# A scan followed by two mixture-of-experts layers: how many empty row blocks the ACT queue writes per unit of work

## The chip, the cores and the metric

The kernel runs on one core of one Trainium2 chip. The metric is the device time of one execution in microseconds (us); lower is better. The core has five engines with an instruction queue each: PE (matrix multiply), DVE (vector), ACT (activations; it also issues DMAs), POOL and SP (which here only issues DMAs). A queue is worked off in order: an instruction that waits holds up everything behind it on that engine.

## What is computed

```python
for t in range(S):                       # x is 2 x 5056 x 256
    h = f[:, t] * h + i[:, t] * x[:, t]  # gated scan, y[:, t] = h
x = y.reshape(10112, 256)
x = moe(x, cosine router, w1, w2)        # layer 0
out = moe(x, linear router, w1, w2)      # layer 1
# moe: expert e = argmax of 8 logits per row, gate = softmax probability of e
#      out[row] = gate * (relu(x[row] @ w1[e]) @ w2[e]),  w1: 256 x 1024, w2: 1024 x 256
```

## The kernel before

**Rows sorted by expert.** Each layer has a table in DRAM, `X[0]` and `X[1]`, with a region for every expert that would hold all rows. The scan and the router of layer 0 write each row, and the router of layer 1 each output row of layer 0, to the next free slot of its expert, by indirect DMAs of POOL. A layer's work is cut into tiles of 128 rows of one expert. The number of rows of an expert is known only at the end, so a layer is planned in phases: while rows still arrive, only full tiles are planned; when the last row has been counted, `checkpoint(..., final=True)` plans the rest, among them one partly filled tile for each expert. What lies behind an expert's last row must then be defined, so for each of the eight experts a block of 128 rows (`zrow`, 129 KB, zeros with an invalid row number) is written just behind its last row. These eight writes per layer are the subject of the change.

**Units.** A tile needs two units, one for each half of the 1024 hidden columns. A unit is `mm1` (L827, 24 matmuls of 128 columns into one PSUM buffer `hps`), `evac` (ACT makes the high half of `hT` with a relu at L835, DVE the low half at L188), and three units later `mm2` (L849, 12 matmuls of 256 columns, `hT` times `W2`, into a PSUM buffer `ops`). Most tiles run their two units one after the other; the last 21 tiles of layer 0 and the first 21 of layer 1 run all first halves and then all second halves, with the partial sum copied out by ACT (`acc`, L853), while the weights of one half are exchanged. Six PSUM buffers are shared by `hps`, `ops`, the scan's transposes and the transposes `x2p` of layer 1's router.

**Order of the work.** Python builds a list of slots, one for each unit; a function put into slot i with a priority writes its instructions there. Within a slot: `do_loads` (1), `mm1` (5), `pad_rows` (13), router steps and weight parts, `evac` (50), `mm2` (55). From slot 17 on the order on PE, ACT, SP and POOL is this written order; that on DVE is chosen by a scheduler when the kernel is built. ACT also loads weights (512 KB each from `w1b`, `w2b` into `ws`, L384, three buffers) and converts them (L397, L419).

**The empty blocks.** `checkpoint` computes the eight addresses on DVE (`pads`), and puts the eight calls into the slots behind its own:

```python
for e in range(E):                                             # E = 8, L715
    at(now[0] + 1 + e // cfg["padn"], 13, pad_rows, m, pads, e)
```

```python
def pad_rows(m, pads, e):                                      # L703
    if e == 0:
        A.load(preg, pads[0:1, 0:E])                           # addresses into ACT's registers
        ...
    x_write(m, A.dma_start(out=X[m][ds(pval[m, e], P), :], in_=zrow[0]), "Xp")
```

`x_write` says what need not be ordered: all other writes to `X[m]` are declared independent of the blocks. The blocks are not declared independent of each other (the address is a register's value), so each block's DMA waits, at ACT, until the one ahead has landed. The loads of tiles that the final plan made (`t_load`, L802, on SP) wait for all eight (`x_read`); tiles of earlier phases don't.

Of the kernel before, what the change touches and what calls it, by code (L numbers as in the profile page):

```python
# [117 lines left out]
 't0at': (-3, 40),  # L118
 'w1at': (16766, 49534),
 'w2at': (82048, 114816),  # L120
 'padn': 1,
 'xq': 'S'}


# [1315 lines left out]
```

## Time and profile before

| | |
|---|---|
| three runs | 1076.33, 1081.48, 1098.4 us; median 1081.48 |
| the profiled execution's own time | 1075.63 us |
| its span, first to last instruction | 1073.8 us |
| busy share of the span: PE, DVE, ACT, POOL | 93%, 56%, 49%, 40% |
| mean granted clock of PE | 0.981 |

How to read it: the span is shorter than the time by 1.83 us around it. The final plan of layer 0 stands at about 425 us of the span, that of layer 1 at about 650 us. PE is busy nearly always, so time is lost or won where PE stands still, and a share of busy time of another engine says little; what counts is whether PE waits for it.

### The profile page before, as it was taken

The page shows a single profiled execution, that of the slowest core. Times are in us where ns is not written, and L with a number is a line of the kernel's source. Part 1 is how long each engine was busy: PE and PEld are TensorE (multiplying, and loading weights), DVE is VectorE, ACT ScalarE, POOL GpSimd, SP SyncE. Part 2 cuts the span into 40 slices and gives each one's busy share as a digit, 9 for nine tenths or more (in the row PEclk, how much of TensorE's full clock was granted, in tenths as well). Part 3 has the DMA queues.
Part 4 walks back from the last instruction along what each step waited for, and adds up shares of the span by engine and source line. Part 5 has one row for each costly group of instructions (what it writes and reads, how often), then busy time and mean ns, then how long its engine had stood idle before and what let it go on. Part 6 is the DMA issues. An engine that isn't in the chain of part 4 may idle for free. (4 is left out here: it accounts for less than half of the span.)

```text
span 1073.8 us, 37047 instructions
## 1 busy us (share of the span) xinstructions
PE 1003.0 (93%) x13267; PEld 933.6 (87%) x13267; DVE 604.3 (56%) x2007; ACT 525.3 (49%) x1301; POOL 432.7 (40%) x864
## 2 busy tenths in 40 slices
PE   4557999999999999889999999899999999999997
PEld 4436889999999998779999998899999999999997
DVE  8989767787778776556429876543222222222221
ACT  6888455655555654456336564543333333333332
POOL 4276756667776665222101551143222222222222
PEclk9967999999999999989999999999999999999999
DMA  9699425876665773555459589843322222222220
GB/s 352 204 331 236 120 68 115 136 142 115 130 134 135 137 120 91 154 156 151 108 113 259 121 173 219 157 100 84 55 55 51 51 51 52 46 52 44 46 51 31
DMA packets 195616, 132.72 MB, mean 124 GB/s; under 512 B 169601, under 2 KB 172558, under 8 KB 195440
## 3 DMA queue, kind: packets, MB, share of 16 engines
q1 hardware_dynamic: 170080, 58.07, 27.5%
q10 hardware_dynamic: 13504, 40.74, 15.3%
q0 software_dynamic: 11856, 31.51, 11.0%
q8 instruction: 118, 1.93, 0.8%
q14 instruction: 58, 0.48, 0.2%
HBM read 58.89 MB, written 38.85 MB: 91 GB/s over the span
## 5 line engine op out<-in xcount | busy, mean ns | idle before, releaser
L827 PE MATMUL hps<-xT,W 128*128 128x128 f16 x7968 | 508.4, 220 | 16.7 <-DVE hT L188 5.8
L827 PEld LDWEIGHTS <-W 128*128 x7968 | 476.5, 98 | 29.5 <-issue 16.3
L849 PE MATMUL ops<-W,hT 128*128 x3984 | 492.5, 273 | 2.8 <-ACT W L397 1.0
L188 DVE SCALAR_TENSOR_TENSOR hT<-hps,hT 128x512 f16<-128x512 f32 x332 | 228.3, 688 | 343.3 <-ACT hT L835 325.9
L849 PEld LDWEIGHTS <-hT 128*128 128x128 f16 x3984 | 375.1, 98 | 44.1 <-issue 4.1
L835 ACT ACTIVATE hT<-hps 128x512 f16<-128x512 f32 x332 | 197.7, 596 | 336.9 <-PE hps L827 258.5
L1017 POOL DMA_INDIRECT out<-osum,ti x83 | 81.3, 979 | 301.2 <-ACT osum L1013 176.6
L995 POOL DMA_INDIRECT X<-trow,tsl x83 | 98.4, 1186 | 49.5 <-DVE tsl L188 16.4
L690 POOL DMA_INDIRECT X<-row,sl x79 | 88.8, 1124 | 69.8 <-issue 25.3
L1013 ACT ACTIVATE osum<-ops,exr 128x256 f32<-128x256 f32 x62 | 29.4, 474 | 47.0 <-PE ops L849 44.8
L196 POOL TENSOR_TENSOR lf<-exr,us 128x2 f32<-128x2 f32 (+1 forms) x42 | 9.5, 226 | 105.2 <-DVE us L192 52.0
L188 DVE SCALAR_TENSOR_TENSOR W<-ws,W 128x1024 f16<-128x1024 f32 x34 | 41.4, 1221 | 7.3 <-ACT W L397 7.2
L531 PE MATMUL yt<-cs,xf 128*128 128x128 f32 x126 | 27.9, 299 | 16.2 <-DVE xf L516 13.6
L516 DVE TENSOR_TENSOR_SCAN xf<-xf 128x256 f32<-128x256 f32 (+3 forms) x64 | 42.7, 708 | 0.1
L397 ACT ACTIVATE W<-ws 128x1024 f16<-128x1024 f32 x35 | 36.9, 1058 | 9.1 <-DMA ws<-w1b 5.0
L872 ACT ACTIVATE trow<-osum 128x256 f16<-128x256 f32 x83 | 35.1, 423 | 12.4 <-DMA X<-trow,tsl 4.9
L861 ACT ACTIVATE osum<-ops 128x256 f32<-128x256 f32 x58 | 22.2, 382 | 35.4 <-PE ops L849 29.0
L188 DVE SCALAR_TENSOR_TENSOR trow<-osum,tsc,trow 128x256 f16<-128x256 f32 x83 | 37.4, 481 | 3.3 <-ACT trow L887 1.7
L533 PEld LDWEIGHTS yt<-cs,xf 128*128 128x128 f32 x252 | 35.3, 204 | 0.8 <-issue 0.7
L188 DVE SCALAR_TENSOR_TENSOR row<-yt,sc,row 128x256 f16<-128x256 f32 x79 | 36.0, 472 | 0.0
L887 ACT ACTIVATE trow<-osum,tsc 128x256 f16<-128x256 f32 x62 | 28.1, 500 | 14.8 <-DVE tsc L193 11.9
L571 ACT ACTIVATE row<-yt,sc 128x256 f16<-128x256 f32 x79 | 33.1, 478 | 3.2 <-DVE sc L193 3.2
(161 smaller groups left out, 956.6 us busy)
## 6 DMA issues: line engine op xcount, KB each, us to landing
xf<-xf ACTq DMA_DIRECT2D x28, 512.0 KB
ws<-w1b ACTq DMA_DIRECT2D x16, 512.0 KB
ws<-w2b ACTq DMA_DIRECT2D x16, 512.0 KB
W<-w1a SPq DMA_DIRECT2D x11, 512.0 KB
W<-xf SPq DMA_DIRECT2D x8, 512.0 KB
ws<-w2a ACTq DMA_DIRECT2D x8, 512.0 KB
WD<-wq SPq DMA_DIRECT2D x8, 512.0 KB
W<-WD SPq DMA_DIRECT2D x8, 512.0 KB
```

Of the source, the lines that this page charges most:

```text
L188: return eng.scalar_tensor_tensor(out=out, in0=in0, scalar=s, in1=in1, op0=op0, op1=op1, **kw)
L397: A.activation(out=hi, in_=src, func=ACTF.Copy, scale=64.0)
L516: V.tensor_tensor_scan(out=t[:, k, lo:hi], data0=t[:, 2 + k, lo:hi], data1=t[:, k, lo:hi], initial=init, op0=ALU.mult, op1=ALU.subtract)
L533: T.matmul(out=yt[:, D:D + E], lhsT=t[:, k, i * P:(i + 1) * P], rhs=ide[:, (1 - k) * (P + E):(1 - k) * (P + E) + E], start=(k == 0), stop= ...
L571: A.activation(out=p["row"][:, o + i, 0:D], in_=yv(d["yt"][i]), func=ACTF.Copy, scale=p["sc"][:, o + i:o + i + 1])
L690: x_write(0, G.indirect_dma_start(out=X[0], out_offset=IndirectOffsetOnAxis(ap=p["sl"][:, i, 0:1], axis=0), in_=p["row"][:, i, :].bitcast( ...
L827: T.matmul(out=hps[:, c, :], lhsT=w, rhs=xt[:, a, :], start=(n == 0), stop=(n == 5))
L835: A.activation(out=hh[:, 0], in_=hps, func=ACTF.Relu)
L849: T.matmul(out=o, lhsT=hT[:, a + k, :], rhs=w[:, b * D:(b + 1) * D], start=(first and k == 0 and n == 0), stop=(last and k == 3 and n == 2))
L872: A.activation(out=d["row"][:, i, D:2 * D], in_=t["O"], func=ACTF.Square, scale=0.25, accum_out=d["ss"][:, i:i + 1])
L995: x_write(1, G.indirect_dma_start(out=X[1], out_offset=IndirectOffsetOnAxis(ap=sl[:, i, 0:1], axis=0), in_=d["row"][:, i].bitcast(I32), in ...
L1017: i = ins_of(G.indirect_dma_start(out=out, out_offset=IndirectOffsetOnAxis(ap=ti, axis=0), in_=r, in_offset=None, bounds_check=N - 1, oob_ ...
```

## The change

One number in the table of settings: the eight blocks of a layer are written four in the first slot behind the final plan and four in the second, not one in each of eight slots. This holds for both layers.

```diff
- 'padn': 1,
+ 'padn': 4,
```

On ACT in layer 0, from the loading of the addresses (`pads`) on, the queue before has one block (`X_99<-zrow`), the high half of `hT` of that unit, two copies of transposes (`x2p`), a weight load and the second block. The names after "waits" are semaphores; DMAHW ones count landed DMAs.

```order
L705 TENSOR_LOAD pads [waits DVE_49]
L708 ISA
L708 DMA X_99<-zrow 128x258 [waits DMAHW4_49]
L835 ACTIVATE hT<-hps 128x512 [waits PE_49]
L923 ACTIVATE x_11125<-x2p 128x512 [waits DMAHW2_49,DMAHW1_49,DMAHW6_49,DMAHW0_49,PE_49]
L923 ACTIVATE x_11127<-x2p 128x512 [waits DMAHW2_49,DMAHW7_49,DMAHW1_49,PE_49]
L384 DMA ws<-w1b 128x1024
L708 ISA
L708 DMA X_99<-zrow 128x258 [waits DMAHW4_49,DMAHW0_49]
```

The same place on ACT now:

```order
L708 DMA X_99<-zrow 128x258 [waits DMAHW4_49]
L708 ISA
L708 DMA X_99<-zrow 128x258 [waits DMAHW6_49,DMAHW4_49]
L708 ISA
L708 DMA X_99<-zrow 128x258 [waits DMAHW6_49,DMAHW0_49]
L708 ISA
L708 DMA X_99<-zrow 128x258 [waits DMAHW1_49,DMAHW0_49]
L835 ACTIVATE hT<-hps 128x512 [waits PE_49]
L923 ACTIVATE x_11128<-x2p 128x512 [waits DMAHW2_49,PE_49]
L923 ACTIVATE x_11130<-x2p 128x512 [waits DMAHW7_49,DMAHW2_49,PE_49]
L384 DMA ws<-w1b 128x1024 [waits DMAHW2_49]
```

Three more blocks stand ahead of `hT`, the two copies and the weight load; four more follow behind that load, ahead of the next unit's `hT`.

On ACT in layer 1, between the first and the second unit behind the plan, the queue before has one block (`X_100<-zrow`) for each `hT`, weight part (L397), weight load (L384) and partial sum (L853).

```order
L835 ACTIVATE hT<-hps 128x512 [waits PE_49]
L397 ACTIVATE W_1_105<-ws 128x4x256 [waits DMAHW0_49]
L384 DMA ws<-w2b 128x1024 [waits DMAHW5_49,DVE_49]
L853 ACTIVATE acc_17990<-ops 128x256 [waits PE_49]
L708 ISA
L708 DMA X_100<-zrow 128x258 [waits DMAHW3_49]
L835 ACTIVATE hT<-hps 128x512 [waits PE_49]
```

The same place on ACT now:

```order
L835 ACTIVATE hT<-hps 128x512 [waits PE_49]
L397 ACTIVATE W_1_105<-ws 128x4x256
L384 DMA ws<-w2b 128x1024 [waits DMAHW1_49,DVE_49]
L853 ACTIVATE acc_17993<-ops 128x256 [waits PE_49]
L708 ISA
L708 DMA X_100<-zrow 128x258 [waits DMAHW0_49]
L708 ISA
L708 DMA X_100<-zrow 128x258 [waits DMAHW4_49,DMAHW3_49]
L708 ISA
L708 DMA X_100<-zrow 128x258 [waits DMAHW7_49,DMAHW4_49]
L708 ISA
L708 DMA X_100<-zrow 128x258 [waits DMAHW7_49]
```

Four blocks stand ahead of the second `hT` where one stood, and as many ahead of the first. On PE, SP and POOL the order of the instructions is the same in both kernels (on PE only buffer numbers differ).

## Rows read from the trace of the kernel before

**Rows 1.** Busy time by engine over the whole span, from the page.
```profile
PE 1003.0 (93%) x13267; PEld 933.6 (87%) x13267; DVE 604.3 (56%) x2007; ACT 525.3 (49%) x1301; POOL 432.7 (40%) x864
```

**Rows 2.** Who waited for the block writes (tile zrow): line, total us, times.
```profile
  ACT hT L835: 17.0, 9
```

**Rows 3.** ACT's timeline, layer 0: start, us, engine, line, [idle before <-releaser]; ACTq issues.
```profile
427.33 0.38 ACTq L708 DMA_DIRECT2D X<-zrow  x1
...
440.15 0.42 ACT L872 ACTIVATE trow<-osum 128x256 f16<-128x256 f32 x1 [2.33 <-DMA X<-zrow]
...
443.29 0.34 ACTq L708 DMA_DIRECT2D X<-zrow  x1
...
443.94 0.35 ACTq L384 DMA_DIRECT2D ws<-w1b  x1
...
444.17 1.08 ACT L923 ACTIVATE x<-x2p 128x512 f16<-128x512 f16 x2
...
445.54 0.34 ACTq L708 DMA_DIRECT2D X<-zrow  x1
...
450.50 0.34 ACTq L708 DMA_DIRECT2D X<-zrow  x1
...
453.16 0.34 ACTq L708 DMA_DIRECT2D X<-zrow  x1
```

**Rows 4.** PE's timeline, layer 0, behind the final plan.
```profile
441.69 0.29 PE L915 MATMUL x2p<-id,trow 128*128 128x128 f16 x2 [0.64 <-DVE toh L188]
...
455.40 0.86 PE L915 MATMUL x2p<-id,trow 128*128 128x128 f16 x8 [1.50 <-ACT trow L887]
...
461.65 2.72 PE L827 MATMUL hps<-xT,W 128*128 128x128 f16 x24 [3.99 <-DMA xT<-X]
464.16 2.76 PE L849 MATMUL ops<-W,hT 128*128 x12
466.72 1.83 PE L827 MATMUL hps<-xT,W 128*128 128x128 f16 x24
```

**Rows 5.** SP's waits, 400 to 480 us: total us, times, longest.
```profile
SPq L802 <- DMA X<-zrow: 24.1, 1, 24.1
```

**Rows 6.** One window: us, busy of PE, PEld, DVE, ACT, POOL, granted clock, DMA share, GB/s.
```profile
462.00:467.00 5.00, 5.00 (x38) 4.20 (x36) 0.69 (x1) 0.63 (x2) 0.14 (x1) 0.50 0.53 102
```

**Rows 7.** ACT's timeline, layer 1.
```profile
656.63 0.36 ACTq L708 DMA_DIRECT2D X<-zrow  x1
...
659.78 1.06 ACT L397 ACTIVATE W<-ws 128x1024 f16<-128x1024 f32 x1 [2.15 <-DMA ws<-w2b]
...
660.74 0.36 ACT L853 ACTIVATE acc<-ops 128x256 f32<-128x256 f32 x1
...
663.15 0.36 ACTq L708 DMA_DIRECT2D X<-zrow  x1
...
668.17 0.39 ACTq L708 DMA_DIRECT2D X<-zrow  x1
...
668.60 0.60 ACT L835 ACTIVATE hT<-hps 128x512 f16<-128x512 f32 x1 [3.23 <-DMA X<-zrow]
...
670.66 0.39 ACTq L708 DMA_DIRECT2D X<-zrow  x1
```

**Rows 8.** PE's timeline, layer 1.
```profile
663.18 1.50 PE L827 MATMUL hps<-xT,W 128*128 128x128 f16 x24
664.52 1.47 PE L849 MATMUL ops<-W,hT 128*128 x12
665.83 1.50 PE L827 MATMUL hps<-xT,W 128*128 128x128 f16 x24
...
669.98 1.50 PE L827 MATMUL hps<-xT,W 128*128 128x128 f16 x24 [1.34 <-DVE hT L188]
...
688.56 1.51 PE L849 MATMUL ops<-W,hT 128*128 x12 [1.01 <-ACT W L397]
```

**Rows 9.** PE's waits, 645 to 700 us: total us, times, longest.
```profile
PE hps L827 <- DVE hT L188: 3.8, 3, 1.9
```

## The prediction

> **What bounds the kernel now.** The busy times come first: PE works 93% of the span, so time is won or lost only where PE stands still [rows 1]. Then I asked who waits for the changed writes: ACT stood before its `hT` activations for 17.0 us, nine times, until a block of empty rows had landed [rows 2]. Does PE feel that? In layer 0, SP's first load of a tile from the final plan waited 24.1 us for the blocks [rows 5], and PE ran out of tiles: it stood 3.99 us until 461.65 [rows 4]. The three groups after that took 2.72, 2.76 and 1.83 us, against 1.50, 1.47 and 1.50 elsewhere [rows 4, 8]: the clock granted from 462 to 467 us was 0.50, that is 1.2 instead of 2.4 GHz, after the stop and full again before 472 or so [rows 6]. The lower level cost 1.22 + 1.29 + 0.33 = 2.84 us. In layer 1 no tile came late, but PE waited 3.8 us, in three places, for `hT` halves that ACT made late [rows 9]; the one at 669.98 goes back to an `hT` at 668.60 that had stood 3.23 us behind a block [rows 7, 8].
>
> So the blocks have two prices: how late the last one lands (SP, layer 0), and how long ACT is held at once. The change lowers the first and raises the second.
>
> **What a block costs ACT.** A block is issued when the one ahead has landed, so the distance of two issues is the price where ACT had nothing else to do. Alone: 445.54 − 443.29 = 2.25, 453.16 − 450.50 = 2.66, 670.66 − 668.17 = 2.49 us [rows 3, 7]. Behind a 512 KB weight load on the same queue: 450.50 − 445.54 = 4.96 (the load was issued at 443.94), and in layer 1, where loads follow each other, 6.52 (656.63 to 663.15) and 5.02 (663.15 to 668.17) [rows 3, 7]. I take 2.5 alone and 4.96 behind a load, and keep 2.66 and 6.52 as the upper end.
>
> The trace's blocks differ by a factor of three at one size. The Trainium skill (DMA: Bandwidth & Descriptors, "Anatomy of one DMA") gives a write about 2.0 us plus its bytes at 436 GB/s; for 129 KB an estimate from that page is 2.30 us for any block. This agrees with the lone rows, and the row of 6.52 us speaks against it. What the rule would make of the time stands among the rivals.
>
> **Layer 0.** The queue up to the first block, 427.33, is unchanged. Three more at 2.5 each: the fourth is issued at 434.83. Issue 0.38, `hT` 0.60, the two `x2p` copies 1.08, weight load issue 0.35: 437.24; the fifth waits for the fourth's landing, 437.33. It stands behind that load: sixth at 442.29, seventh 444.79, eighth 447.29. Behind it stand the square of one output tile (0.42), two `hT` (1.20) and a copy (taken as 0.36, like `acc`), with the issue 0.38: the second square starts at 449.7 [rows 3, 7]. In the trace of before the second square starts at 440.15, and PE's transposes that need its row at 441.69, 1.54 us later [rows 3, 4]. So they start at 451.2: **+9.5 us**. Everything else PE has in between (about one unit, and the router's logits that wait for the copies) fits before that. PE stands still longer than before 461.65, so I add the lower clock once: +2.84.
>
> What goes: the eighth block lands near 450 to 452 instead of after 453.16, and PE reaches the first tile of the final plan some 9 us later. Its stop of 3.99 us goes, with the 2.84 us of clock behind it, and the 1.50 us at 455.40, where ACT's `trow` had waited for the last block [rows 4]. Net: 9.5 + 2.84 − 3.99 − 2.84 − 1.50 = **+4.0 us**.
>
> **Layer 1.** A new matmul group into `hps` needs the buffer of the group three units ahead (six buffers, two used by a unit). The wait at 669.98 shows the distance: `hT` at 668.60 on ACT, 1.38 us until PE starts (ACT 0.60, then DVE's half) [rows 7, 8]. First block 656.63, behind a load as before, so the second at 663.15; third 665.65, fourth 668.15. The `hT` behind it starts at 668.53, and PE's group of 663.18 starts at 669.91. Then ACT has `hT` 0.60, a weight part 1.06, a load issue 0.35 and `acc` 0.36: 670.90, by when the fourth has landed. Fifth 670.90, behind that load; sixth 675.86, seventh 678.36, eighth 680.86. The second `hT` starts at 681.24, and PE's group of 665.83 starts at 682.62: **+16.8 us**. The lower clock of the first stop is swallowed by the second; behind the second it costs 2.84. The 3.84 us of `hT` waits later on (1.34 + 1.91 + 0.59, [rows 9]) go, since no block is left. The 1.01 us at 688.56, where PE waited for a weight part [rows 8], I leave as it is. Net: 16.8 + 2.84 − 3.84 = **+15.8 us**.
>
> At nothing I cost the earlier loads of SP, which stood 24.1 us there before [rows 5], and the later place that the scheduler gives DVE's half of `hT` in layer 0: it still comes while PE waits for the router's rows.
>
> **Sum.** 4.0 + 15.8 = 19.8 us. The profiled execution took 1075.63 us, which gives 1095.4. The median of the three runs is 5.85 us above it, the lowest 0.7; so I put the time at 1098, a little above the sum.
>
> With the upper prices (2.66 alone, 6.52 behind a load) layer 0 gives 437.97, 444.49 and 449.81 for the fifth, sixth and eighth block, so 453.75 and +6.6 net; layer 1 gives 671.2, 677.7 and 683.1, so 684.8 and +18.0. Sum 24.6: 1100.2, and with the median's 5.85 about 1106.
>
> **Rivals.**
>
> *A load ahead costs a block nothing.* The fifth blocks then take 2.5 us like the others: transposes of layer 0 at 448.8 (+1.6 net), PE's group of layer 1 at 680.2 (+13.3 net), sum 14.9, 1090.5 us. For it: ACT's loads are paused while it stands, so less is in flight. Against it: 4.96 and 6.52 in the trace [rows 3, 7].
>
> *Every block has one price, and it is that of the shortest row.* With 2.25 us for each block, the first of layer 1 too: layer 0's transposes at 447.2 (no change net), layer 1's group at 674.6 (+7.8 net), 1083.4 us. The row of 2.25 speaks for it, that of 6.52 against it [rows 3, 7]. By the Trainium skill's 2.30 us (same page and section) it would be an estimated 1084.0.
>
> *The weights become late.* Five weight loads of layer 1 stand behind the second group of blocks, each converted two units (2 x 2.65 = 5.30 us by the starts 663.18 and 665.83) after its issue [rows 8]. If each takes as long as the first block, 6.52, PE loses 1.22 us at each: +6.1, so 1101.5 on the profile's own time. For it: the 1.01 us at 688.56. Against: one load at a time is lighter than three.
>
> *The other side: ACT's stop is hidden.* If the four blocks of a group went out without waiting for each other, ACT would be held for four issues of 0.38, and only the gain would stay: 3.99 + 2.84 + 1.50 + 3.84 = 12.2 us, 1063.5, not slower. It decides at the point where three distances and an issue fit into PE's lead: in layer 1 the `hT` in question could start at 663.18 − 1.38 = 661.8, 5.2 us after the first block, so a distance would have to be under 1.6 us. The shortest in the trace is 2.25 [rows 3]. And ACT's 3.23 us before 668.60 show that such a wait holds ACT itself [rows 7].
>
> **How the numbers follow.** The forecast (blocks at 2.25 to 2.66 us alone, near 5 us behind a load) gets 0.60, its own range being 1091 to 1106; weights late 0.15; the load costing nothing 0.12; one price 0.08; the other side 0.05. Two per cent, about what a measurement of this kernel can tell from no change, is 21.6 us, and the sum lies just under it. Of the forecast I put two in five above it, with most of the late weights, and something for the scatter of the runs: slower 0.40, within 2% 0.58, faster 0.02 (even the other side is 1.1% only). The range goes from the one price, 1083, to the upper prices and the late weights on the runs' median, 1109.
>
> **What would show it.** In the changed kernel's trace: SP's wait for the blocks under 24.1 us, and PE's stop of 3.99 us before the first final tile gone; ACT idle for blocks some 34 us in all (by the distances above, less the issues), against 17.0 before `hT`; issues of blocks 2.5 us apart, and about 5 where a weight load went ahead; PE waiting for `trow` in layer 0 some 8 us and for `hT` in layer 1 twice, near 7 and 7 to 10 us, each followed by a granted clock of 0.50. I am wrong if blocks of a group are issued well under 2 us apart, if PE's stops are under half of that, or if PE waits for weight parts behind 688 by more than a microsecond.

## The result, and the profile after

| | before | after |
|---|---|---|
| median, us | 1081.36 (6 runs, 1076.28 to 1098.4) | 1095.65 (6 runs, 1090.96 to 1097.08) |
| ratio, 95% interval | 1 | 1.0137 [1.0098, 1.0176] |
| the profiled execution, us | 1075.63 | 1095.75 |

The change costs 14.3 us by the medians (1.37% by the ratio): it is measurably slower, but by less than the 2% that the chances counted with. The ratio is formed from executions in the faster of two states, so the one of 1098.4 us does not enter it.

Where did the profiled execution's 20.1 us come from? Three distances between block issues cut the span, the same points in both kernels: up to the first block of layer 0 (427.33 before, 432.66 after), from there to the first block of layer 1 (229.30 and 234.87), and from there to the end (417.17 and 426.47). The differences are +5.33, +5.57 and +9.30 us. The first third comes ahead of any changed instruction. In this pair of executions the change itself thus cost 14.87 us. That this meets the ratio's 1.37% of 1081 (14.8) so closely is chance: a second profile of the changed kernel ("the changed kernel again" below, on another chip) has 425.78, 229.83 and 428.4 us for the three stretches, which against the same profile of before is −1.55, +0.53 and +11.2. So what lies ahead of the first block goes either way. The share of layer 1 is well known: in the four profiles that have dependent groups of four there it is +9.3, +11.2, +11.6 and +9.7. That of layer 0 is not: +5.6, +0.5, +3.7 and +3.2, and with one block per unit, as before, the same stretch took 226.56 us in another execution ("layer 1 alone").

Busy time of the engines after, from the page, answering to [rows 1]: PE does 3.5 us more, a clock effect, since its instructions are as many; ACT does no more than before. The span grew by 20.2 us, so PE stands still longer.

```profile
PE 1006.5 (92%) x13267; PEld 936.3 (86%) x13267; DVE 604.1 (55%) x2007; ACT 524.2 (48%) x1301; POOL 429.4 (39%) x864
```

Who waited for the blocks (line, total us, times), answering to [rows 2]. Before, ACT waited 17.0 us ahead of `hT`, and besides ahead of `trow`:

```profile
  ACT trow L872: 3.4, 2
```

These eleven short waits of 20.4 us have become three long ones of 29.5:

```profile
  ACT hT L835: 19.6, 2
  ACT trow L872: 9.9, 1
```

SP's wait for the blocks between 400 and 480 us, answering to [rows 5]: 24.1 us at a stretch before, now 16.8 in five pieces, the longest 6.6. This is the gain that the change brings.

```profile
SPq L802 <- DMA X<-zrow: 16.8, 5, 6.6
```

ACT's timeline, layer 0 (around 440) and layer 1 (around 680), answering to [rows 3, 7]; start, us, engine, line, idle before and what released it. An `ACTq ... x4` row is a group: its time goes from the first issue to the end of the fourth.

```profile
432.66 8.03 ACTq L708 DMA_DIRECT2D X<-zrow  x4
...
440.73 0.60 ACT L835 ACTIVATE hT<-hps 128x512 f16<-128x512 f32 x1 [8.66 <-PE hps L827]
...
440.95 0.35 ACTq L384 DMA_DIRECT2D ws<-w1b  x1
...
443.28 8.78 ACTq L708 DMA_DIRECT2D X<-zrow  x4
...
452.18 0.42 ACT L872 ACTIVATE trow<-osum 128x256 f16<-128x256 f32 x1 [9.87 <-DMA X<-zrow]
...
666.06 0.34 ACTq L384 DMA_DIRECT2D ws<-w2b  x1
...
667.53 11.34 ACTq L708 DMA_DIRECT2D X<-zrow  x4
...
678.92 0.60 ACT L835 ACTIVATE hT<-hps 128x512 f16<-128x512 f32 x1 [11.59 <-DMA X<-zrow]
...
679.02 0.35 ACTq L384 DMA_DIRECT2D ws<-w2b  x1
...
681.21 7.53 ACTq L708 DMA_DIRECT2D X<-zrow  x4
...
688.78 0.60 ACT L835 ACTIVATE hT<-hps 128x512 f16<-128x512 f32 x1 [8.05 <-DMA X<-zrow]
```

Each group holds ACT: the activation behind it was ready and stood 8 to 12 us. (At 440.73 the last releaser by the profile is PE, but the group's fourth block was issued at 440.35, so ACT could not have come much earlier. In the second profile of the changed kernel the view puts this hold down to the blocks too, and ACT's waits for them sum to 37.9 us; the prediction had 34.) What PE made of it shows in its timeline, answering to [rows 4, 8]:

```profile
455.53 1.34 PE L915 MATMUL x2p<-id,trow 128*128 128x128 f16 x8 [7.47 <-ACT trow L887]
...
456.67 2.77 PE L849 MATMUL ops<-W,hT 128*128 x12
...
459.33 2.20 PE L827 MATMUL hps<-xT,W 128*128 128x128 f16 x24
461.42 1.47 PE L849 MATMUL ops<-W,hT 128*128 x12
...
680.29 2.72 PE L827 MATMUL hps<-xT,W 128*128 128x128 f16 x24 [7.98 <-DVE hT L188]
...
682.81 2.76 PE L849 MATMUL ops<-W,hT 128*128 x12
...
690.15 2.72 PE L827 MATMUL hps<-xT,W 128*128 128x128 f16 x24 [4.58 <-DVE hT L188]
...
692.67 1.61 PE L849 MATMUL ops<-W,hT 128*128 x12
```

The releaser names `trow` and `hT`, DVE or ACT; the chain back from each of them ends at an ACT activation that stood behind a group of blocks. The stop for `xT` before the first final tile (3.99 us, [rows 4]) is in no row of after, and neither is the 1.01 us for a weight part [rows 8]. The `hT` waits of [rows 9] were three of 3.8 us; now (645 to 700 us) they are two:

```profile
PE hps L827 <- DVE hT L188: 12.6, 2, 8.0
```

Behind each stop the granted clock is low. Windows of layer 0 and of layer 1 (columns as in [rows 6]): 0.50, the level of 1.2 GHz, in the 5 us behind the stop that ends at 455.53, 0.92 in the next five; 0.50 in the window behind the stop that ends at 680.29; 0.66 in the window that contains the end of the last stop, at 690.15.

```profile
455.00:460.00 5.00, 4.34 (x29) 3.30 (x30) 3.53 (x11) 4.54 (x11) 2.48 (x7) 0.50 0.82 195
460.00:465.00 5.00, 5.00 (x75) 4.79 (x73) 1.60 (x5) 1.33 (x3) 2.39 (x3) 0.92 0.26 89
...
680.00:685.00 5.00, 4.71 (x35) 4.04 (x35) 1.46 (x2) 0.73 (x2) 0.00 (x0) 0.50 0.65 156
688.00:693.00 5.00, 2.85 (x26) 2.78 (x26) 3.29 (x5) 4.22 (x9) 0.00 (x0) 0.66 0.59 143
```

### The profile page after: what moved, and what is told of

Its sections match the earlier page's. It is cut to its first block, busy times and chain, and to the rows that moved or that the text cites. A ratio compares the mean times of both kernels' runs of the same rounds, so it can differ in the third digit from the quotient of the medians.

```text
span 1094.0 us, 37050 instructions
## 1 busy us (share of the span) xinstructions
PE 1006.5 (92%) x13267; PEld 936.3 (86%) x13267; DVE 604.1 (55%) x2007; ACT 524.2 (48%) x1301; POOL 429.4 (39%) x864
## 3 DMA queue, kind: packets, MB, share of 16 engines
q10 hardware_dynamic: 13504, 40.74, 14.8%
## 5 line engine op out<-in xcount | busy, mean ns | idle before, releaser
L995 POOL DMA_INDIRECT X<-trow,tsl x83 | 98.8, 1190 | 52.4 <-DVE tsl L188 16.8
L397 ACT ACTIVATE W<-ws 128x1024 f16<-128x1024 f32 x35 | 37.1, 1063 | 12.6 <-DMA ws<-w1b 6.2
L861 ACT ACTIVATE osum<-ops 128x256 f32<-128x256 f32 x58 | 22.2, 382 | 36.7 <-PE ops L849 29.7
L887 ACT ACTIVATE trow<-osum,tsc 128x256 f16<-128x256 f32 x62 | 28.1, 500 | 18.2 <-DVE tsc L193 12.2
```

Of the source, the lines that this page charges most:

```text
L397: A.activation(out=hi, in_=src, func=ACTF.Copy, scale=64.0)
L995: x_write(1, G.indirect_dma_start(out=X[1], out_offset=IndirectOffsetOnAxis(ap=sl[:, i, 0:1], axis=0), in_=d["row"][:, i].bitcast(I32), in ...
```

## The experiments

The theory: a block waits at ACT for the landing of the one ahead, so four in a row hold ACT for four landings, and PE stands as soon as that is longer than its lead. Its rivals: the loss doesn't come from the groups' hold of ACT but from the place, or from the transfers themselves when they come close together, or from the order on DVE, which the scheduler chooses anew for each kernel; the loss of layer 1 is a consequence of the displaced layer 0; the time ahead of the first block belongs to the change. Three chips were used, each with its own runs of the kernel before; ratios, not times, are compared between them.

| run | blocks per unit | blocks wait for each other | median, us | ratio [95%] |
|---|---|---|---|---|
| first chip, kernel before | 1 | yes | 1083.57 | 1 |
| layer 0 alone | 4 in layer 0, 1 in layer 1 | yes | 1088.36 | 1.0050 [1.0010, 1.0091] |
| layer 1 alone | 1 in layer 0, 4 in layer 1 | yes | 1094.27 | 1.0091 [1.0057, 1.0124] |
| four, independent | 4 | no | 1073.23 | 0.9895 [0.9864, 0.9926] |
| one, independent | 1 | no | 1077.82 | 0.9936 [0.9898, 0.9974] |
| second chip, kernel before | 1 | yes | 1071.96 | 1 |
| eight | 8 | yes | 1092.84 | 1.0198 [1.0167, 1.0229] |
| two | 2 | yes | 1085.66 | 1.0123 [1.0076, 1.0170] |
| four with small activations | 4 | yes | 1087.92 | 1.0161 [1.0139, 1.0184] |
| eight, independent | 8 | no | 1066.94 | 0.9950 [0.9916, 0.9985] |
| third chip, kernel before | 1 | yes | 1074.72 | 1 |
| the changed kernel again | 4 | yes | 1086.94 | 1.0122 [1.0082, 1.0163] |
| four, independent, again | 4 | no | 1063.36 | 0.9912 [0.9877, 0.9947] |
| eight, independent, again | 8 | no | 1063.73 | 0.9901 [0.9867, 0.9935] |

**One layer at a time.** The change is made in one layer and left out in the other:

```diff
- at(now[0] + 1 + e // cfg["padn"], 13, pad_rows, m, pads, e)
+ at(now[0] + 1 + e // cfg["padn"][m], 13, pad_rows, m, pads, e)
- 'padn': 4,
+ 'padn': (4, 1),        # layer 0 alone;  (1, 4): layer 1 alone
```

Layer 0 alone:

> Four blocks per unit in layer 0 alone, layer 1 as before. Between the two profiles PE fell back by 5.3 us before the first block was issued, where both programs are the same, by 5.6 us more between the first block of layer 0 and that of layer 1, and by 9.3 us from there to the end. If each layer pays for its own blocks, this gives before + 5.6, some 1087 us. Rival: the fall-back ahead of the blocks belongs to the change after all (another order of building shifts the start), then it is here as well: before + 11, 1092 us.

Measured: 1.0050 [1.0010, 1.0091], some 5 us. Its PE timeline has the stop at the router's transposes and no stop for `xT`; in layer 1 PE's waits for `hT` are 3.9 us in three places, as in the kernel before:

```profile
454.91 1.34 PE L915 MATMUL x2p<-id,trow 128*128 128x128 f16 x8 [6.29 <-ACT trow L887]
```

Layer 1 alone:

> Four blocks per unit in layer 1 alone. If each layer pays for its own: before + 9.3, some 1091 us, and with the run of layer 0 alone the two add up to the changed kernel's + 14. Rival: what layer 1 lost came from its being reached later or from loads displaced in layer 0; then under + 5 here.

Measured: 1.0091 [1.0057, 1.0124], some 10 us. The stop for `xT` in layer 0 is there as before (4.3 us), and PE's two waits in layer 1 are those of the changed kernel (645 to 700 us):

```profile
PE hps L827 <- DVE hT L188: 12.3, 2, 7.7
```

The two excesses add up: 0.50 + 0.91 = 1.41%, against 1.37 for both at once, each with an interval of 0.3 to 0.4 to either side. Within these, each layer pays for its own groups; layer 1 doesn't suffer from layer 0's displacement, and nothing need come from ahead of the first block.

**The blocks no longer wait for each other.** The writes stay where they are, but are declared independent of each other, which they are: each lies in the region of another expert. So that two independent writes don't stand directly behind each other in the written order, each has a one-element activation ahead of it:

```diff
 def x_write(m, i, group="Xw"):
-        if group == "Xw" and pval:
+        if group == "Xp" or pval:
             tc.declare_no_dep(i, group=f"Xp{m}", reason="disjoint rows")
 def pad_rows(m, pads, e):
+        d = sm.tile([1, 1], F32, name="gap", tag="gap", bufs=1)
+        A.activation(out=d, in_=c64[0:1, 0:1, 0], func=ACTF.Copy)
```

> The changed kernel with the eight blocks declared independent of each other (their rows are disjoint), so that a block is issued without the landing of the one ahead; a one-element activation on ACT stands ahead of each block, since the order written by hand keeps neighbours dependent. Theory (ACT is held by each block's wait for the one ahead): blocks some 0.6 us apart, no stop of PE at the transposes of layer 0 or at hT in layer 1, and the stops of before gone as well (3.99 + 2.84 + 1.50 + 3.84 = 12.2 us): 1069 us. Rival (the cost is eight writes and earlier tile loads crowded into two units, or the order on DVE, not the wait): as the changed kernel, 1094 to 1096 us.

Measured: 0.9895 [0.9864, 0.9926], 11 us *faster* than the kernel before. ACT's timeline of this run in layer 0: the four issues of the first group stand 0.53 to 0.58 us apart, where they stood 2.18 to 2.88 apart in the changed kernel. Not every issue is that quick: in layer 1 three of the six distances within the groups are 1.86, 2.01 and 1.23 us, and the runs don't show why.

```profile
432.43 0.38 ACTq L710 DMA_DIRECT2D X<-zrow  x1
433.01 0.36 ACTq L710 DMA_DIRECT2D X<-zrow  x1
433.56 0.34 ACTq L710 DMA_DIRECT2D X<-zrow  x1
434.09 0.34 ACTq L710 DMA_DIRECT2D X<-zrow  x1
```

ACT's 29.5 us of waiting shrink to one wait of 1.7 (who waited for `zrow`):

```profile
  ACT gap L709: 1.7, 1
```

PE has no stop for `trow` or `xT` in layer 0, and one of 1.0 us for `hT` in layer 1. The same bytes are written at the same places in the order, and closer together, so it is neither the transfers nor the place that costs, but the wait of one for the other.

The order on DVE is a rival that these runs settle for layer 1 alone. By the traces of all the runs it differs from that of the kernel before in at most 39 of 2007 places, every one of them in layer 0 (between 426 and 463 us); in layer 1 it is the same in all. "Layer 1 alone" and "one, independent" even have the order of the kernel before throughout, and still cost 0.91% and gain 0.64%. In layer 0 the groups and the order on DVE change together; that the groups are what costs there rests on the trace, where PE's longest stop goes back to a `trow` of ACT that had stood 9.87 us behind a block.

The small activations are a second edit in that kernel. The control keeps them and the dependence:

> The changed kernel with the one-element activation ahead of each block, the blocks dependent as before: the control for the independent blocks. Theory: the activations stand in ACT's wait and cost nothing, 1094 to 1097 us. Rival (the activation itself, by changing the order on DVE or the place of the waits, brought the gain): under 1085.

Measured: 1.0161 [1.0139, 1.0184], as slow as the changed kernel (1.0122 and 1.0137, overlapping intervals). ACT's waits for the blocks are back, now mostly at the small activations that stand between them, and so are PE's for `hT` (13.1 us, twice):

```profile
  ACT gap L709: 26.8, 10
  ACT hT L837: 5.3, 3
  ACT trow L874: 1.9, 1
```

The activations are not what made the kernel fast.

The same with one block in each unit, the kernel before with the declaration alone:

> The kernel before (one block per unit in eight units) with the blocks declared independent of each other. Theory: ACT's 20 us of waits for blocks go, and with them 1.50 + 3.84 us of PE; the eighth block is issued eight units (21 us) after the first, so near 449 on the clock of before instead of 453, lands some 3 us later, ahead of PE's need at 457.7, so most of 3.99 + 2.84 goes too: 1070 to 1075 us. Rival (waits of ACT were covered): no change, 1081 us.

Measured: 0.9936 [0.9898, 0.9974]. The waits for `hT` in layer 1 are gone (0.4 us left), but the stop for `xT` stayed, which I had expected to go for the most part. PE's waits from 400 to 480 us:

```profile
PE hps L827 <- DMA xT<-X: 3.9, 1, 3.9
```

The reason is in the order, not in the waits: spread over eight units, the eighth block goes out 22.2 us after the first (439.73 to 461.92), and SP still waits 20.9 us for it. So the two prices are separate. Independence takes away the hold of ACT; only moving the blocks forward takes away the wait of SP. Four, independent, has both: SP's wait is 4.7 us.

**More and fewer per unit.** One number is changed:

```diff
- 'padn': 4,
+ 'padn': 8,        # eight;  2: two
```

> All eight blocks in one unit, each waiting for the one ahead. By the distances of the changed kernel's trace (2.4 us in layer 0; 5.8 and then 2.5 us in layer 1) ACT's first hT behind the blocks comes 17 us after the first block in layer 0 and 21 us after it in layer 1, so in layer 1 PE resumes at the time at which it resumes in the changed kernel behind its second stop, with one unit less done (2.7 us, up to 5.4 at the lower clock), and in layer 0 with about one unit less done. Theory (the time of ACT's wait less PE's lead counts): the changed kernel + 5 to 8 us, 1100 to 1104. Rival (each stop of PE has its price, and one long stop is cheaper than two): the changed kernel less 4 to 7 us, 1088 to 1092.

Measured for eight: 1.0198 [1.0167, 1.0229], 4.9 us above the control with four on the same chip. ACT's timeline has the group of eight in one piece, in layer 0 and in layer 1:

```profile
429.54 16.64 ACTq L708 DMA_DIRECT2D X<-zrow  x8
...
662.62 19.95 ACTq L708 DMA_DIRECT2D X<-zrow  x8
```

and PE's timeline one stop for each, in layer 0 at the router's logits and in layer 1 at `hT`:

```profile
447.37 0.22 PE L931 MATMUL lp<-wg,x 128*128 128x16 f16 x2 [11.49 <-ACT x L923]
...
683.99 2.72 PE L827 MATMUL hps<-xT,W 128*128 128x128 f16 x24 [16.56 <-DVE hT L188]
```

This is just under the 5 to 8 us that I had expected. A longer group holds ACT longer and stops PE longer; the rival, that getting the blocks over with sooner makes up for it, falls.

> Two blocks per unit in four units, each waiting for the one ahead. Theory: in layer 1 the chain of eight takes some 23 us (5.8, then 2.5 to 3.2 each), against PE's lead and four units; PE stands some 10 us in three or four shorter stops, less of it at the lower clock: layer 1 before + 6 to 8; layer 0 before + 2 to 4: 1090 to 1094 us, between the kernel before and the changed one. Rival (short stops are hidden by PE's lead, only a stop of three and more waits shows): within 3 us of before, 1081 to 1085.

Measured for two: 1.0123 [1.0076, 1.0170], 13.7 us, a little more than I had expected and about what the changed kernel costs with four (1.0137, and 1.0122 in a repetition below). A group of two already exceeds the lead where a load is ahead: its first group in layer 1 takes 9.06 us (ACT's timeline), the first block alone 8.70.

```profile
657.65 9.06 ACTq L708 DMA_DIRECT2D X<-zrow  x2
```

In this profile PE also waits for `trow` (9.9 us), for `hT` (7.0, three times), for `acc` (2.6) and for a weight part (2.4): groups of two come in four units each, and their stops fall on more places. That price and group size go together linearly was not shown: two and four can't be told apart.

**A version that beats both kernels.** All eight in one unit, independent:

> All eight blocks in one unit, independent of each other (with the one-element activation ahead of each). Theory (only the waits cost, the writes and their issue don't): as the four independent blocks, 1070 to 1075 us; ACT is held for 8 x 0.6 = 5 us, which PE's lead of 5 to 8 us just covers. Rival (many writes at once delay the loads of weights and tiles): 1078 or more.

Measured: 0.9950 [0.9916, 0.9985]; PE's largest stop for the blocks is 2.0 us, where eight dependent ones cost 11.49 and 16.56. The gain of 5 us lies between the theory (6 to 11 us under the kernel before) and the rival (some 3 at most), and its interval reaches into both. Is four or eight better? The two and the changed kernel once more on one chip:

> The changed kernel itself beside the two with independent blocks, on one chip: again 1.0 to 1.8% over before by its earlier interval.

> Four independent blocks per unit, a second time, beside eight per unit: 0.7 to 1.4% under before by its earlier interval.

> Eight independent blocks in one unit beside four per unit on the same chip. If ACT's issue time counts once it passes PE's lead (8 x 0.6 = 5 us and the first block's wait), eight are 2 to 5 us slower than four. If only waits count, the two are within 2 us of each other.

Measured: the changed kernel 1.0122 [1.0082, 1.0163], four independent 0.9912 [0.9877, 0.9947], eight independent 0.9901 [0.9867, 0.9935]. On this chip the gain is in the theory's range. Once independent, four and eight are alike (0.4 us apart), and both are about 1% faster than the kernel before and 2% faster than the changed one.

Moving the blocks to another engine's queue was not tried.

## Why the prediction was right, and where its sum was off

The forecast, two groups that hold ACT for longer than PE's lead, holds: 1095.65 lies in its own range, 1091 to 1106, and a change within 2% is what I gave 0.58. The mechanism is shown: ACT stands behind the groups, PE behind ACT, and without the wait of one block for the other the loss is gone. The sizes are less good than the time suggests. The rival "a load ahead costs a block nothing" had a sum of 14.9 us, which is what was measured (14.87 in the profiles), where mine had 19.8; but it has +1.6 for layer 0 and +13.3 for layer 1, against +5.57 and +9.30, so that it meets the sum is chance too. The other side (the group goes out without waiting, 1063.5) falls for this kernel by the distances of 1.88 to 5.80 us, but its arithmetic was good: it forecast −12.2 us for blocks that don't wait, and four independent ones give −11.4 and, repeated, −9.5 by the ratios.

By the steps:

- **Price of a block alone, 2.5 us.** In the changed kernel 2.88, 2.63, 2.18, 2.36, 1.92 in layer 0 and 2.78, 2.42, 2.64, 1.88 in layer 1. Right in the mean (2.41); a single one can be longer, 3.93 in the second profile (layer 0, the block from 428.10 to 432.03). The Trainium skill (DMA: Bandwidth & Descriptors, "Anatomy of one DMA — SWDGE (gpsimd) path") gives its fit for DMAs that GpSimd issues, while ACT issues these, so the estimate of 2.30 us carries it over to another path. That estimate agrees with the mean of these rows. It doesn't agree with the 4.15 and 5.80 us behind loads, and the time that it would give, 1084.0, is 12 us too low.
- **Layer 0, stop.** Forecast: transposes 23.87 us after the first block; measured 455.53 − 432.66 = 22.87, so +8.5 instead of +9.5. PE's wait: forecast about 8, measured 7.47. The block behind the load took 4.15, not 4.96.
- **Layer 0, what goes.** The stop of 3.99, the clock behind it and the 1.50 for `trow` all went. The lower clock behind the new stop cost 0.48 (transposes, 1.34 against 0.86) + 1.30 + 0.70 = 2.48 us, against 2.84. By these terms the net would be 8.5 + 2.5 − 3.99 − 2.84 − 1.50 = +2.7, while from block to block it is +5.57 in this profile, and +3.7 with layer 0 alone. Of the 2.9 us between, 1.6 stand in two small waits of PE between the layers (1.1 and 1.0, before 0.3 and 0.2); whether the change causes these isn't known, and the rest is open. It is within the scatter: in the second profile of the changed kernel the same distance is +0.53.
- **Layer 1, first stop.** Forecast: `hT` 11.90 us after the first block, PE 13.28; measured 678.92 − 667.53 = 11.39 and 680.29 − 667.53 = 12.76. Right; the first block took 5.80 instead of 6.52.
- **Layer 1, second stop: the term that was mis-sized.** I let the fifth block take 4.96 us, because a weight load goes out ahead of it. It took 2.66, and 2.8 to 3.2 in the three other profiles with such groups in layer 1. The first block was 0.72 shorter as well. So the second `hT` came 21.25 us after the first block, not 24.61, PE resumed after 22.62, not 25.99, and the term is 22.62 − 9.20 = +13.4 instead of +16.8. Here the rival "a load ahead costs a block nothing" was right, for this one block. The lower clock behind that stop cost 1.22 + 0.14 = 1.36 us instead of 2.84; but behind the same stop it cost 2.91 in the second profile and 2.65 with layer 1 alone, so this term was not wrong, it varies from execution to execution.
- **Layer 1, what I left as it is.** The 1.01 us for a weight part went. Net by the terms: 13.4 + 1.36 − 3.84 − 1.01 = +9.9; the trace has +9.30; forecast +15.8. The rival of the late weights falls with it: PE waits for no weight part up to 715 us.

So the sum of 19.8 us was too large by 5: by 6.5 in layer 1, less 1.6 by which it was too small in layer 0. That it met the profiled execution (1095.4 against 1095.75) is chance: that execution was 5.33 us late before the first block was issued. That my 1098 came near the median of 1095.65 is chance as well: the sum stood on an execution 5.7 us faster than the median before, 1081.36, and this made up for the 5 us too many; on the median the sum would have given 1101.

Why the load cost the fifth block 4 to 5 us in most profiles of layer 0 (4.15 here, 4.72 with layer 0 alone, 4.02 in the control, but 2.94 in the second profile) and hardly anything in layer 1 isn't settled. How long ago the load went out doesn't explain it: here it was 2.33 us ahead of the block in layer 0, which took 4.15, and 2.19 ahead in layer 1, which took 2.66; in the kernel before, layer 1 has a block 2.16 us behind its load that took 4.93.

The kernel before could have warned me that 4.96 was one value of several. Two other blocks of its layer 0 stood behind a load and took 3.85 (432.97 to 436.82) and 3.52 us (439.77 to 443.29, the latter in [rows 3]):

```profile
432.42 0.34 ACTq L384 DMA_DIRECT2D ws<-w1b  x1
...
432.97 0.36 ACTq L708 DMA_DIRECT2D X<-zrow  x1
...
436.82 0.36 ACTq L708 DMA_DIRECT2D X<-zrow  x1
...
437.25 1.55 ACTq L384 DMA_DIRECT2D ws<-w1b  x1
439.77 0.34 ACTq L708 DMA_DIRECT2D X<-zrow  x1
```

## What to carry to other kernels

A DMA whose issue waits for the landing of another holds the queue of the engine that issues it, and with it everything that this engine computes for others: put such a DMA in a group only if the group's landings together are shorter than the consumer's lead, here about 5 us against 7.5 to 11.3 for four. When a tool orders writes that can't overlap, because their addresses are register values, declare them independent first and group them then: groups of four alone cost 1.2 to 1.4%, independence alone gave 0.6%, both gave 0.5 to 1.1%. And read a chain of single issues in the trace by the distances of the issues: they are the price per link.

## What the runs showed of the hardware that I had not expected

- The same 129 KB write took between 1.77 and 8.70 us until the next could be issued, longest for the first block of layer 1 (5.3 to 8.7 in the eight profiles in which the blocks wait for each other), where weight loads had gone out ahead of it; I had counted with 2.25 to 6.52.
- Eight of them in a chain hold an engine for 16.64 us in layer 0 and 19.95 us in layer 1 (issues included); eight independent ones go out in 5.7 to 7.3 us.
- The first block of layer 0 was issued anywhere between 425.5 and 439.7 us in the thirteen profiles, although PE, ACT, SP and POOL have the same order of instructions up to there (but for the small activation in some). A place in the span can't be compared, nor the time of a single execution to better than some 5 us. Distances between two points of the same execution are safer over a few units, but not over hundreds of us: from the first block of layer 0 to that of layer 1 the changed kernel took 234.87 us in one execution and 229.83 in another.
- In the kernels before and after, each stop of PE of 4.0 to 8.0 us was followed by the clock's lower level. What that cost did not follow the length of the stop: 2.84 us behind 3.99, 2.48 behind 7.47, 1.36 behind 4.58; and behind the same last stop of layer 1 1.36 in one profile and 2.91 in another.
